# A gated recurrence and a gated convolution on one core: norms kept side by side as word pairs, a written-out order for every engine, and tile-sized loads

## The chip, the cores and the metric

The kernel runs on one NeuronCore of a Trainium2 chip. Its time is the device time of one execution in microseconds (us). A core has five engines that run side by side, each with its own queue of instructions, worked off in order: PE (TensorE, matrix products and transposes), DVE (VectorE), ACT (ScalarE), POOL (GpSimd) and SP (SyncE, which here only issues transfers). Transfers between main memory and the on-chip memory (SBUF) run on 16 DMA engines. PE writes into PSUM[...].

## The reference

There are 4 sequences of 6336 tokens with 256 channels; all inputs and the output are fp32.

```python
a_base = sigmoid(a_param)
a_t    = exp(8 * sigmoid(r_gate) * log(clip(a_base)))
norm   = sqrt(max(1 - a_t * a_t, 1e-6))
h      = a_t[:, t] * h + norm * sigmoid(i_gate) * x     # over t, per sequence
gate   = sigmoid(causal convolution of h, 5 taps per channel)
out    = (gate * (h @ w_val)) @ w_out
```

So each of the 25,344 tokens needs three loads of 256 values, one store of 256 values, a recurrence along the sequence, a convolution and two products with 256x256 matrices.

## The kernel before

**Tiles and chunks.** The tokens of all four sequences stand in one row. A *tile* is 512 tokens (three are 256), a *chunk* is two tiles (some chunks at both ends are one tile). There are 51 tiles and 28 chunks (`CHUNKS`, L17). The 256 channels are two halves of 128, `h` = 0 and 1. Data arrive with tokens on the partitions; the recurrence needs channels on the partitions, so data are transposed on PE.

**One tile's way through the engines.** The names are those of the functions `op_...`:

| step | engine | what it does |
|---|---|---|
| load, loadx | SP | r and i gates, and x, of one chunk |
| tanh | ACT | tanh of half of both gates of a tile, to bf16 `tring` |
| u2 | DVE or POOL | (1 + tanh i) * x to bf16 `uring`; one instruction on DVE (L360), two on POOL (L363, L364); the string `U2` says which |
| srT, exp | PE, ACT | transpose of the r part by half chunk; a = exp(...) to fp32 `aring` |
| e | POOL | a * a to fp32 `ering` (L384) |
| sq | ACT | norm = sqrt(0.25 - 0.25 a * a), bf16, written over `ering` (L388), for one to three chunks at once (`UNITS`) |
| nT, xg | PE, DVE | transpose of the norms back to tokens (L397); `uring` times norm (L404) |
| xT, scan | PE, DVE | transpose of `uring` (L332); the recurrence over a half chunk (L425) |
| conv, tg | PE, ACT | five taps as products with diagonal matrices (L451); tanh (L459) |
| val, gv | PE, DVE | product with w_val (L467); (1 + tanh) * val (L477) |
| out, osb, store | PE, DVE or ACT, SP | product with w_out by 256 tokens (L489); copy from PSUM (L500, L502; the string `OSB` says which); store |

The functions sq and the others on ACT need different tables, so every batch of norms costs a table load before it and one after it (ACT_TABLE_LOAD).

**What sets the order.** The program is made by a planner. `make_jobs` (L110) lists all steps with an engine, a cost (`COST`) and the steps that they wait for. `make_plan` (L160) then goes through time: it takes the step that can start first by these costs, and among equals the one with the lowest `PRIO`. It also hands out the four shared PSUM banks (srT, nT, xT, out). The kernel issues the steps in the order that comes out, so each engine has a fixed queue. SP's queue holds all loads and stores in one order; one that waits for a buffer or for its data holds up all behind it.

**Buffers.** r and i gates: `NIN` = 2 chunks (four tiles); x: `NX` = 3 chunks (six tiles); tanh outputs: `NTR` = 3 and `NTI` = 5 tiles; `ering` 8 tiles, `aring` and `uring` 10, `yring` 6.

**Which tokens lie where.** r is loaded so that a partition holds four neighbouring tokens of a tile, 4 KB in one piece. i and x are loaded with token k * 128 + p on partition p, pieces of 1 KB. The exp turns the order of r into plain token order when it writes `aring`.

Of the kernel before, what the change touches and what calls it, by code (L numbers as in the profile page):

```python
# [9 lines left out]
P = 128  # L10
# [8 lines left out]
UNITS = [1, 2, 2, 3, 3, 3, 3, 3, 2, 2, 1, 3]  # L19
# [4 lines left out]
NIN = 2  # L24
NX = 3
NTR = 3
NTI = 5
# [5 lines left out]
OSB = ("ADDDDDDDDDDDDADDDDDDDDDDDDADDDDDDDDADDDDDDDDDADDDDAADDADDDDDDADDADDDDAADDAAADADADADADADADA"  # L33
       "DAAAAAAAA")

U2 = "PDPDDDDDDPDPDPDPDDPDPPPPPPPPPPPPPPPDPPPPPPPDPPPPPPP"

COST = dict(load=(0.05, 2.8), loadx=(0.02, 1.5), tanh=(0.2, 1.7), u2P=(0.25, 3.15), u2D=(0.2, 1.55), srT=(0.05, 0.45), exp=(0.35, 0.86), e=(0.1, 1.8),
            sq=(0.3, 1.71), nT=(0.05, 0.47), xg=(0.1, 0.58), xT=(0.05, 0.45), scan=(0.21, 2.14), conv=(0.2, 1.1), tg=(0.19, 0.83),
            val=(0.02, 0.93), gv=(0.15, 1.07), out=(0.02, 0.47), osbD=(0.68, 0), osbA=(0.59, 0),  # L40
            store=(0.05, 1.3))
PRIO = dict(load=5.92, loadx=5.97, store=2.53, tanh=6, exp=2.8, sq=0.42, tg=-0.32, srT=-1.6, nT=0.31, xT=3.79,
            conv=5.3, val=4.34, out=2.99, e=5.93, u2=6, xg=4.55, scan=0.36, gv=-0.61, osb=-0.99)
# [66 lines left out]
def make_jobs(sh):  # L110
# [3 lines left out]
    jobs = {op: [] for op in PRIO}  # L114
# [8 lines left out]
    for g, (_, n) in enumerate(sh.tiles):  # L123
        f = n / WIN
        c = sh.chunk_of[g]
        job("tanh", "ACT", f, [("load", c), ("u2", g - NTI)]
            + ([("srT", 2 * sh.chunk_of[g - NTR] + 1)] if g >= NTR else []))
        job("u2", "DVE" if U2[g] == "D" else "POOL", f, [("tanh", g), ("loadx", c)] + ([("xT", 2 * sh.chunk_of[g - NU] + 1)] if g >= NU else []), "u2" + U2[g])
# [7 lines left out]
    for c, (_, n, g0, g1) in enumerate(sh.chunks):  # L136
        f = n / CHUNK
        job("load", "DMA", 2 * f, [("tanh", sh.chunks[c - NIN][3] - 1 if c >= NIN else -1)])
        job("loadx", "DMA", 2 * f, [("u2", sh.chunks[c - NX][3] - 1 if c >= NX else -1)])
# [20 lines left out]
def make_plan(sh):  # L160

    jobs = make_jobs(sh)
    reads = dict(exp="srT", xg="nT", scan="xT", osb="out")
    nxt = dict.fromkeys(jobs, 0)
    done, free, order, mode = {}, dict(DMA=START, ACT=ACT_START), [], "E"
    bank_free, banks = [0.0] * BANKS, {}
    while True:
        best = None  # L170
        for op, todo in jobs.items():
            i = nxt[op]
            if i == len(todo):
                continue
            eng, dur, deps, need = todo[i]
            t = free.get(eng, 0.0)
            if need:
                b = min(bank_free)
                if b == math.inf:
                    continue  # L180
                if b:
                    t = max(t, b + SEM)
            for d in deps:
                e = done.get(d)
                if e is None:
                    break
                if e + SEM > t:
                    t = e + SEM
            else:
                if best is None or (t, PRIO[op]) < best[:2]:  # L190
                    best = (t, PRIO[op], op, i, eng, dur, need)
        if best is None:
            break
        t, _, op, i, eng, dur, need = best
        if eng == "ACT" and op != "osb":
            if (op == "sq") != (mode == "S"):
                dur += TABLE
            mode = "S" if op == "sq" else "E"
        free[eng] = t + dur
        done[op, i] = t + dur + (DMA_LAT if eng == "DMA" else 0.0)  # L200
        if need:
            banks[op, i] = bank_free.index(min(bank_free))
            bank_free[banks[op, i]] = math.inf
        if op in reads:
            bank_free[banks[reads[op], i]] = t + dur
        order.append((t, op, i, eng, dur))
        nxt[op] += 1
    assert all(nxt[op] == len(todo) for op, todo in jobs.items()), nxt
    order.sort(key=lambda o: o[0])
    return order, banks  # L210
# [3 lines left out]
def kernel(  # L214
# [29 lines left out]
    def load(c):  # L244
        t0, nt, g0, g1 = chunks[c]
        nw, nj = g1 - g0, nt // (g1 - g0) // P
        ri = inp.tile([P, 2, 2, SUB, D], FP32, name="ri", tag="ri", bufs=NIN)

        nc.sync.dma_start(ri[:, 0, 0:nw, 0:nj, :], rf[t0:t0 + nt, :].rearrange("(w p j) d -> p w j d", w=nw, j=nj))
        nc.sync.dma_start(ri[:, 1, 0:nw, 0:nj, :].rearrange("p w j d -> p (w j) d"),  # L250
                          if_[t0:t0 + nt, :].rearrange("(k p) d -> p k d", p=P))
        live["ri", c] = ri

    def loadx(c):
        t0, nt, g0, g1 = chunks[c]
        xt = inp.tile([P, 2 * SUB, D], FP32, name="xt", tag="xt", bufs=NX)
        nc.sync.dma_start(xt[:, 0:nt // P, :], xf[t0:t0 + nt, :].rearrange("(k p) d -> p k d", p=P))
        live["xt", c] = xt

    with tc.manual_schedule():  # L260
# [57 lines left out]
        def bank(b, dtype):  # L318
            return psum.tile([P, WIN * 4 // mybir.dt.size(dtype)], dtype, name=f"bank{b}", tag=f"bank{b}", bufs=1)
# [24 lines left out]
        def op_tanh(g, eng):  # L344
# [3 lines left out]
            if g == chunks[c][3] - 1:  # L348
                del live["ri", c]
# [195 lines left out]
```

## Time and profile before

| | |
|---|---|
| median of 13 runs | 319.63 us (317.71 to 324.51) |
| the profiled execution | 317.76 us, span from first to last instruction 316.0 us |
| TensorE clock granted | 0.984 |
| moved | 104.55 MB in 67,327 packets, 54,238 of them between 512 B and 2 KB |
| mean rate of transfers | 331 GB/s; 395 GB/s in the best of 40 slices |
| chain that ended last | ACT 25%, DVE 23%, PE 18%, DMA 17%, issue 12% |
| POOL idle before the square e, waiting for exp | 51.0 us |
| SP waiting for output copies on DVE | 113.2 us |

How to read the lines in the next part. The first lines give, by engine, busy us, share of the span and number of instructions (PEld is the weight loads of PE). A row of 40 digits has the busy share of 40 equal slices of the span in tenths, 9 being 90% or more. A line of the waits reads: engine and line, what it waited for, us in total, number of times, longest. A group of instructions has line, engine, operation, output and inputs, shapes and types, count, then busy us and mean ns of one, then the idle time of the engine just before them and what ended it. A line of the timeline has start, duration, engine, line and operation, and how many instructions were put together. Instructions on one engine overlap a little: the mean of one can be longer than the distance from one start to the next. A busy PE is not a PE at its peak, because the records include the way through the array.

### The profile page before, as it was taken

The page shows a single profiled execution, that of the slowest core. Times are in us where ns is not written, and L with a number is a line of the kernel's source. Part 1 is how long each engine was busy: PE and PEld are TensorE (multiplying, and loading weights), DVE is VectorE, ACT ScalarE, POOL GpSimd, SP SyncE. Part 2 cuts the span into 40 slices and gives each one's busy share as a digit, 9 for nine tenths or more (in the row PEclk, how much of TensorE's full clock was granted, in tenths as well). Part 3 has the DMA queues.
Part 4 walks back from the last instruction along what each step waited for, and adds up shares of the span by engine and source line. Part 5 has one row for each costly group of instructions (what it writes and reads, how often), then busy time and mean ns, then how long its engine had stood idle before and what let it go on. Part 6 is the DMA issues. An engine that isn't in the chain of part 4 may idle for free.

```text
span 316.0 us, 7194 instructions
## 1 busy us (share of the span) xinstructions
PE 243.5 (77%) x2954; PEld 161.5 (51%) x2987; DVE 269.0 (85%) x269; ACT 289.8 (92%) x231; POOL 225.2 (71%) x140
## 2 busy tenths in 40 slices
PE   1273778697578759897989698939977997999994
PEld 1142645454445437554655375617754665655562
DVE  3025598999698989999999999987998999999892
ACT  6689999998979999999999999799989999998963
POOL 6328732879478627999999999999996289868000
PEclk9999998999979999999999999997999999999999
DMA  8999999999999999999999999996999994753334
GB/s 207 345 364 380 367 368 378 378 363 372 389 351 355 375 359 374 350 395 383 375 384 389 391 368 394 392 382 184 394 385 396 383 357 161 247 201 129 136 155 179
DMA packets 67327, 104.55 MB, mean 331 GB/s; under 512 B 3287, under 2 KB 54238, under 8 KB 67294
## 3 DMA queue, kind: packets, MB, share of 16 engines
q1 hardware_dynamic: 65904, 103.82, 92.1%
q0 software_dynamic: 1376, 0.26, 1.0%
q8 instruction: 23, 0.38, 0.5%
q14 instruction: 10, 0.08, 0.1%
q10 hardware_dynamic: 14, 0.01, 0.0%
HBM read 78.39 MB, written 25.95 MB: 330 GB/s over the span
## 4 chain that ended last, share of the span: by engine, by line
ACT 25%; DVE 23%; PE 18%; DMA 17%; issue 12%; SPq 1%; ACTq 0%; DVEq 0%
DVE yring L425 13%; DMA ri<-in_i_gate_dram 12%; ACT tring L351 7%; PE gp L451 6%; DVE gv L477 6%; ACT ering L388 6%; ACT tg L459 5%; PE bank L489 5%; DMA xt<-in_x_dram 3%; ACT aring L376 3%; PE bank L397 3%; PE bank L332 2%; DVE osb L500 2%; ACT L459 2%; ACT L388 2%
## 5 line engine op out<-in xcount | busy, mean ns | idle before, releaser
L384 POOL TENSOR_TENSOR ering<-aring 128x1024 f32<-128x1024 f32 (+2 forms) x56 | 97.7, 1764 | 53.9 <-ACT aring L376 51.0
L425 DVE TENSOR_TENSOR_SCAN yring<-aring,yring,bank 128x1024 bf16<-128x1024 f32 (+5 forms) x54 | 110.0, 2050 | 0.8 <-PE bank L332 0.7
L351 ACT ACTIVATE tring<-ri 128x2048 bf16<-128x2048 f32 (+1 forms) x51 | 93.8, 1869 | 7.5 <-DMA ri<-in_i_gate_dram 6.6
L364 POOL TENSOR_TENSOR uring<-t,xt 128x1024 bf16<-128x1024 f32 (+1 forms) x36 | 83.7, 2324 | 9.4 <-DMA xt<-in_x_dram 5.7
L451 PE MATMUL gp<-yring,diag 64*64 64x512 bf16 (+15 forms) x1196 | 68.4, 350 | 5.8 <-ACT tg L459 3.9
L489 PE MATMUL bank<-wo,gv 128*128 128x256 bf16 x396 | 58.0, 281 | 18.8 <-DVE gv L477 8.5
L477 DVE SCALAR_TENSOR_TENSOR gv<-tg,val 128x1024 bf16<-128x1024 bf16 (+1 forms) x54 | 60.2, 1120 | 7.6 <-ACT tg L459 4.7
L376 ACT ACTIVATE aring<-bank,khf 128x1024 f32<-128x1024 bf16 (+2 forms) x56 | 59.6, 1113 | 2.4 <-PE bank L332 1.7
L459 ACT ACTIVATE tg<-gp 128x1024 bf16<-128x1024 f32 (+1 forms) x51 | 51.2, 1004 | 7.5 <-PE gp L451 7.3
L489 PEld LDWEIGHTS <-gv 128*128 128x128 bf16 x396 | 36.2, 100 | 38.3 <-issue 16.7
L467 PE MATMUL val<-yring,wv 128*128 128x512 bf16 (+1 forms) x171 | 47.1, 379 | 3.1 <-DVE gv L477 1.1
L500 DVE COPY osb<-bank 128x512 f32<-128x512 f32 x69 | 45.4, 677 | 2.7 <-PE bank L489 2.1
L451 PEld LDWEIGHTS <-diag 64*64 64x64 bf16 x1196 | 30.8, 108 | 33.1 <-issue 16.8
L388 ACT ACTIVATE ering<-ering,b 128x2048 bf16<-128x2048 f32 (+4 forms) x15 | 46.7, 3112 | 0.3
L332 PE MATMUL bank<-ident_b,tring 128*128 128x128 bf16 x396 | 30.7, 230 | 18.8 <-ACT tring L351 13.5
L404 DVE TENSOR_TENSOR uring<-bank,uring 128x1024 bf16<-128x1024 bf16 (+1 forms) x51 | 33.3, 667 | 11.4 <-PE bank L397 11.2
L397 PE MATMUL bank<-ident_b,ering 128*128 128x128 bf16 x396 | 31.0, 231 | 15.4 <-ACT ering L388 11.5
L363 POOL TENSOR_SCALAR t<-tring 128x1024 f32<-128x1024 bf16 (+1 forms) x36 | 40.1, 1114 | 2.6 <-ACT tring L351 1.1
L332 PEld LDWEIGHTS <-tring 128*128 128x128 bf16 x396 | 25.5, 103 | 27.9 <-ACT tring L351 15.1
L397 PEld LDWEIGHTS <-ering 128*128 128x128 bf16 x396 | 26.3, 104 | 22.6 <-ACT ering L388 14.2
L332 PE MATMUL bank<-ident_b,uring 128*128 128x128 bf16 x396 | 30.6, 226 | 3.2 <-DVE yring L425 2.0
L332 PEld LDWEIGHTS <-uring 128*128 128x128 bf16 x396 | 25.8, 101 | 9.5 <-issue 6.5
(32 smaller groups left out, 110.0 us busy)
## 6 DMA issues: line engine op xcount, KB each, us to landing
out_dram<-osb SPq DMA_DIRECT2D x48, 512.0 KB, 6.6
ri<-in_r_gate_dram SPq DMA_DIRECT2D x23, 1024.0 KB, 8.0
ri<-in_i_gate_dram SPq DMA_DIRECT2D x23, 1024.0 KB, 10.8
xt<-in_x_dram SPq DMA_DIRECT2D x23, 1024.0 KB, 10.2
ri<-in_r_gate_dram SPq DMA_DIRECT2D x2, 512.0 KB, 7.0
ri<-in_i_gate_dram SPq DMA_DIRECT2D x2, 512.0 KB, 8.3
xt<-in_x_dram SPq DMA_DIRECT2D x2, 512.0 KB, 8.2
ri<-in_r_gate_dram SPq DMA_DIRECT2D x3, 256.0 KB, 3.1
```

Source lines behind the costliest of these rows:

```text
L332: nc.tensor.transpose(out=dst[:, col:col + P], in_=src[:, j, h * P:(h + 1) * P], identity=ident_b[:])
L351: nc.scalar.activation(out=tring[:, r:i + 1:i - r, 0:nj, :], in_=ri[:, :, w, 0:nj, :], func=ACT.Tanh, scale=0.5)
L364: nc.gpsimd.tensor_tensor(out=u, in0=t1, in1=xt, op=ALU.mult)
L376: nc.scalar.activation(out=aring[:, h, a0:a0 + nt].rearrange("c (w p j) -> c w p j", p=P, j=nj), in_=live.pop(("srT", k))[:, 0:nt].rearran ...
L384: nc.gpsimd.tensor_tensor(out=ering[:, h, e0:e0 + nt], in0=a, in1=a, op=ALU.mult)
L388: nc.scalar.activation(out=nring[:, :, 2 * e0:2 * e0 + m], in_=ering[:, :, e0:e0 + m], func=ACT.Sqrt, scale=-0.25, bias=b025[:, 0:1])
L397: nc.tensor.transpose(out=nT[:, j, h * P:(h + 1) * P], in_=nring[:, h, n0 + j * P:n0 + (j + 1) * P], identity=ident_b[:])
L425: nc.vector.tensor_tensor_scan(out=yring[:, h, y0 + c0:y0 + c1], data0=aring[:, h, a0 + c0:a0 + c1], data1=xT[:, c0:c1], initial=0.0 if fr ...
L451: nc.tensor.matmul(out=gp[64 * h:64 * h + 64, m, c0:c1], lhsT=diag[rows, h, kk, rows], rhs=yring[rows, h, src:src + c1 - c0], start=(sh == 0),
L459: nc.scalar.activation(out=tg[:, :, 0:nt], in_=live.pop(("gp", g))[:, :, 0:nt], func=ACT.Tanh, scale=0.5)
L477: nc.vector.scalar_tensor_tensor(out=gv[:, 0:nj, hs, :].rearrange("c j h p -> c j (h p)"), in0=tg[:, hs, 0:nt].rearrange("c h (p j) -> c j ...
L489: nc.tensor.matmul(out=ops[:, e * D:(e + 1) * D], lhsT=gv[:, 2 * i + e, hk, :], rhs=wo[:, hk, :], start=(hk == 0), stop=(hk == H - 1))
```

## The change

The change has four parts.

**Loads by tile, 4 KB in one piece.** load and loadx now take one tile. All three inputs are laid out with four neighbouring tokens on a partition. `NIN` is 3 tiles, `NX` 5 tiles, `NTI` 6. Eight load steps instead of six are issued ahead of everything else.

```diff
-    def load(c):
...
-        nc.sync.dma_start(ri[:, 1, 0:nw, 0:nj, :].rearrange("p w j d -> p (w j) d"),
-                          if_[t0:t0 + nt, :].rearrange("(k p) d -> p k d", p=P))
...
+    def load(g):
+        t0, nt = tiles[g]
+        nj = nt // P
+        ri = inp.tile([P, 2, SUB, D], FP32, name="ri", tag="ri", bufs=NIN)
+        for k, src in enumerate((rf, if_)):
+            nc.sync.dma_start(ri[:, k, 0:nj, :], src[t0:t0 + nt, :].rearrange("(p j) d -> p j d", j=nj))
```

**Pairs of tokens as one fp32 word.** With this layout two neighbouring tokens of a channel can be one 4-byte word. `uring` holds pairs of bf16 values, so u2 writes them interleaved: on DVE as two instructions per tile whose sources alternate between two tokens, on POOL as one instruction whose output steps by two elements. The transposes nT and xT then move fp32 words, four per tile and half instead of eight; nT reads every second word, xT writes every second word. `ering` is one row in which the two halves of a chunk stand one after the other, so that sq works on one contiguous stretch.

```diff
-                nc.vector.scalar_tensor_tensor(out=u, in0=ti, scalar=1.0, in1=xt, op0=ALU.add, op1=ALU.mult)
+                xk = xt.rearrange("p (w e) d -> p w d e", e=2)
+                tk = ti.rearrange("p (w e) d -> p w d e", e=2)
+                for k in range(nj // 2):
+                    nc.vector.scalar_tensor_tensor(out=u[:, k], in0=tk[:, k], scalar=1.0, in1=xk[:, k], op0=ALU.add,
+                                                   op1=ALU.mult)
...
-            nc.gpsimd.tensor_tensor(out=u, in0=t1, in1=xt, op=ALU.mult)
+            nc.gpsimd.tensor_tensor(out=u.rearrange("p w d e -> p w e d"), in0=t1.rearrange("p (w e) d -> p w e d", e=2),
+                                    in1=xt.rearrange("p (w e) d -> p w e d", e=2), op=ALU.mult)
...
-                nc.scalar.activation(out=nring[:, :, 2 * e0:2 * e0 + m], in_=ering[:, :, e0:e0 + m],
+                nc.scalar.activation(out=nring[:, 2 * H * e0:2 * H * e0 + H * m], in_=ering[:, H * e0:H * (e0 + m)],
...
-                for j in range(nt // P):
-                    nc.tensor.transpose(out=nT[:, j, h * P:(h + 1) * P],
-                                        in_=nring[:, h, n0 + j * P:n0 + (j + 1) * P], identity=ident_b[:])
+                for w in range(nw):
+                    nc.tensor.transpose(out=nT[:, w * D + h * P:w * D + (h + 1) * P],
+                                        in_=ering[:, n0 + w:n0 + nw * P:nw], identity=ident_f[:])
...
-            transposes(xT, [(uring[:, g % NU], tiles[g][1] // P) for g in range(*chunks[c][2:])], h)
...
+                for w in range(nw):
+                    nc.tensor.transpose(out=xT[:, at + w:at + nw * P:nw],
+                                        in_=uring_w[:, g % NU, w * D + h * P:w * D + (h + 1) * P], identity=ident_f[:])
```

**The order written out.** `PRIO` and the search in time are gone. Five strings (`ORDER`) give the sequence of steps of each engine, one letter a step, and a sixth (`BANK_ORDER`) the PSUM bank of each step that needs one; `make_plan` only works out start times for them. `UNITS`, `OSB`, `U2` and `COST` have new values.

```diff
-UNITS = [1, 2, 2, 3, 3, 3, 3, 3, 2, 2, 1, 3]
+UNITS = [3, 2, 3, 3, 3, 3, 2, 3, 1, 2, 3]
...
-U2 = "PDPDDDDDDPDPDPDPDDPDPPPPPPPPPPPPPPPDPPPPPPPDPPPPPPP"
+U2 = "DDDPDDPDPPPDPDPDPPPPPPPPPPPPPPPPPPPPPPPPPPPPPPPPPPP"
...
+ORDER = dict(
+    DMA=("lllllxlxlxllxxxlxxlxlxxxlslxllslxxxlxlssxlxlxslsxxssllslxxllxsslsllxsxxxsllslsxlxlsxsllssxxlxlxsxsxl"
...
+    ACT=("tteeetteeettqeetttgeetgeqtegtgteetgeettgqetgetgetteegtetgqgetgetgtegettegetgqgettegetgtegetetgqegett"
```

The counts of instructions that follow from it: table loads on ACT 20 instead of 24 after the setup; square roots 14 instead of 15; output copies 71 on DVE and 28 on ACT instead of 69 and 30; u2 on DVE 17 half-tile instructions (8.5 tiles) instead of 15 tiles; u2 on POOL 42 instead of 36; transposes 396 bf16 and 396 fp32 instead of 1188 bf16; load and store issues 204 instead of 135.

**The factor 0.5 of w_out.** The scaling of `wo` in the setup (L313) is gone; the output copies multiply by 0.5 instead (`tensor_scalar` on DVE, an activation with scale on ACT).

```diff
-        nc.vector.tensor_scalar(out=wo[:], in0=wo[:], scalar1=0.5, scalar2=None, op0=ALU.mult)
...
-                nc.vector.tensor_copy(out=dst, in_=ops[:])
+                nc.vector.tensor_scalar(out=dst, in0=ops[:], scalar1=0.5, scalar2=None, op0=ALU.mult)
             else:
-                nc.scalar.copy(out=dst, in_=ops[:])
+                nc.scalar.activation(out=dst, in_=ops[:], func=ACT.Copy, scale=0.5)
```

## The prediction

> **What bounds the kernel now.** I read the engine shares first, then the slices, then the waits, then single stretches of the timeline.
>
> ```profile
> PE 243.5 (77%) x2954; PEld 161.5 (51%) x2987; DVE 269.0 (85%) x269; ACT 289.8 (92%) x231; POOL 225.2 (71%) x140
> ...
> DVE  3025598999698989999999999987998999999892
> ACT  6689999998979999999999999799989999998963
> ...
> DMA  8999999999999999999999999996999994753334
> ```
>
> Three resources are full at once: ACT from slice 4 to slice 38, the transfers until the last load has landed (about 278 us), DVE from slice 7 to the end. The chain of waits agrees: no engine holds more than a quarter of it (ACT 25%, DVE 23%, PE 18%, DMA 17%). So a saving on one engine counts only as far as the others follow. ACT is the fullest: from its first gate tanh at 5.32 us to the end of its last output copy at 312.60 us are 307.3 us; 289.8 - 2.9 (setup) = 286.9 of them are busy and 20.4 idle. The rest, 3.4 us, is the last store. What ACT waits for:
>
> ```profile
> ACT tg L459 <- PE gp L451: 7.3, 10, 1.8
> ACT tring L351 <- DMA ri<-in_i_gate_dram: 6.6, 4, 3.0
> ```
>
> **What leaves ACT.** The order of the new program has 20 table loads in the main part instead of 24 (11 batches of norms instead of 12, two pairs of them without a switch between; the first batch alone is now three chunks), 28 output copies instead of 30, and 14 square-root instructions instead of 15.
>
> ```profile
> L388 ACT ACT_TABLE_LOAD x12 | 15.4, 1283 | 0.2
> ```
>
> 4 x 1.283 = 5.1; 2 x 0.585 (the mean of ACT's copies) = 1.2; one square-root overhead, about 0.2 (6144 elements take 5.416, 2048 take 2.003, so 0.3 is fixed). ACT sheds 6.5 us. The copy that now also multiplies by 0.5 reads the same 128x512 PSUM tile; I cost it at nothing (the tanh of 1024 elements, 1.030, has a scale too), bounds -0.1 to +0.1 us each, 3 us at most.
>
> **ACT's idle time.** Loads go from a chunk (1 MB each of r and i, two chunks in flight) to a tile (512 KB, three tiles in flight); x from three chunks to five tiles. The largest load wait, 3.0 us before the second tanh, is a wait behind earlier transfers at the start and stays in part. Two more, 1.57 and 1.36 us at 203.8 and 231.5, come out of SP's queue: x loads stand before the gate loads and wait for a buffer.
>
> ```profile
> 204.90 10.61 SPq L257 DMA_DIRECT2D xt<-in_x_dram  x2
> 215.61 2.29 SPq L507 DMA_DIRECT2D out_dram<-osb  x2
> 218.00 0.52 SPq L249 DMA_DIRECT2D ri<-in_r_gate_dram  x1
> ```
>
> With tile-sized buffers a slot is free after one tile instead of two. Against it: 153 load issues instead of 84, at about 0.4 us each 28 us more of SP; SP spent 113 us waiting for output copies alone, so that is hidden. SP is still first in, first out: a store that waits holds the loads behind it. I let 4 us of the 20.4 go, and keep the 7.3 us on the convolution. Bounds: 10 us of idle in all, or 30 if three tiles are too few.
>
> Sum on ACT: 5.3 + (286.9 - 6.5) + 16.4 + 3.4 = **305.5 us of span**.
>
> **What is late next: DVE.** Its first real block starts late, because the first large batch of norms comes late:
>
> ```profile
> 30.46 2.86 ACT L388 ACTIVATE ering<-ering,b 128x3072 bf16<-128x3072 f32 x1
> 36.84 6.92 DVE L425 TENSOR_TENSOR_SCAN yring<-aring,yring,bank 128x512 bf16<-128x512 f32 x4
> ```
>
> In the new order ACT does tanh of tiles 0 to 5 and the exps of chunks 0 to 2 (1.05 + 5 x 1.8 + 1.0 + 1.5 + 2.3 = 14.9 us), then the first batch (1.28 + about 3.2). From 5.3 us, with 3 us of load waits, that is 28 us: xg starts at about 29 instead of 34.4. The early batch of chunk 0 (0.72, with two table loads) is gone, so the few DVE operations before 20 us move to after it; DVE had 10 us idle in 20 to 40. Also gone is the scaling of wo (0.29), before which DVE stood 8.6 us; nothing else was ready then, so I count nothing. 71 output copies instead of 69: +1.4.
>
> u2 on DVE falls from 15 whole tiles to 8.5, but each becomes two instructions whose two sources jump 256 elements at every element:
>
> ```profile
> L360 DVE SCALAR_TENSOR_TENSOR uring<-tring,xt 128x1024 bf16<-128x1024 bf16 x15 | 23.2, 1548 | 7.4 <-DMA xt<-in_x_dram 7.4
> ```
>
> By this row: 8.5 x (1.548 + 0.14 for the second instruction, from xg's 683 and 412 ns) = 14.3, a gain of 8.9. The Trainium skill ("Vector Engine (DVE) Microarchitecture Reference", section 5.2, Measured stream behaviour on trn2) speaks against it: a port keeps its rate only on pairs of adjacent words, and with both sources hopping every element a column takes 1.76 ns instead of 1.05. That is +0.72 us on 1024: 8.5 x 2.41 = 20.5, a gain of 2.7. No row here hops like that on two SBUF sources, so I take 2.7. DVE: 269.0 - 2.7 - 0.3 + 1.4 = 267.4; less about 10 before 29 us, plus 15 idle (18.6 now after 36.8) and 4.6 after its last gv: 29 + 257.4 + 15 + 4.6 = 306. DVE and ACT agree within a microsecond; neither lets the other gain more.
>
> **POOL** takes over 6.5 tiles of u2.
>
> ```profile
> 273.37 3.75 POOL L384 TENSOR_TENSOR ering<-aring 128x1024 f32<-128x1024 f32 x2
> 277.08 1.05 POOL L363 TENSOR_SCALAR t<-tring 128x1024 f32<-128x1024 bf16 x1
> 278.21 2.36 POOL L364 TENSOR_TENSOR uring<-t,xt 128x1024 bf16<-128x1024 f32 x1
> 280.53 1.05 POOL L384 TENSOR_TENSOR ering<-aring 128x512 f32<-128x512 f32 x1
> ```
>
> A tile's u2 takes 280.53 - 277.08 = 3.45, two squares 3.75: +22 us on 225, in gaps (POOL waits 51 us for ACT's exp). From tile 16 on all u2 are POOL's: 2 x 3.45 + 3.75 = 10.65 per chunk, against ACT's 280.4 / 24.75 = 11.3. The cover is thin: 0.34 us per tile. The new write puts bf16 elements 4 bytes apart; reads stay contiguous. No row shows such a write: bounds -0.1 to +1.2 (half of 2.36 more); I take +0.1, since bytes and instruction count stay.
>
> **PE** does 396 transposes of fp32 words in place of 792 of bf16.
>
> ```profile
> 161.95 1.27 PE L451 MATMUL gp<-yring,diag 64*64 64x512 bf16 x20
> 163.16 1.05 PE L489 MATMUL bank<-wo,gv 128*128 128x256 bf16 x8
> 164.04 1.06 PE L332 MATMUL bank<-ident_b,uring 128*128 128x128 bf16 x16
> 164.93 1.06 PE L332 MATMUL bank<-ident_b,tring 128*128 128x128 bf16 x16
> ...
> 3.49 0.28 PEld L305 LDWEIGHTS wc_ps<-ident_f,wrow 5*128 5x128 f32 x2 [1.20 <-DMA wrow<-in_moe_conv_w_dram]
> ```
>
> Start to start, a tile costs 1.21 (conv) + 0.88 (out) + 0.99 (val, from three in 0.74) + 24 x 0.056 = 4.42 us, 219 in all; the 243.5 busy counts latency. The nearest row for fp32 is L305: 0.14 per load of 128 columns. At p = 0.14 a tile is 4.42 - 0.90 + 8 x 0.14 = 4.64, 230 in all, under ACT's 5.66 and hidden. Low end 0.056. High end: the skill ("FP8 and Floating Point Precision", TensorE Precision Notes) has true fp32 as four passes, 4 x 0.056 + 0.14 = 0.36, though "TensorE: Matmul & The Clock Gate" (Terms) calls transpose mode four times faster for fp32. No row streams 128 fp32 columns, so both ends stay; I take 0.14, since L305 is one matmul record per transpose. PE decides from p = 0.27.
>
> **Transfers.** Bytes stay 103.8 MB; i and x packets grow from 1 to 4 KB, r and stores are at 4 KB already. At the best slice rate seen, 395 GB/s, all is moved in 263 us, against 277 at the 375 typical here: enough for ACT's pace (4.19 MB per 11.3 us, 371 GB/s), so I count no gain of its own.
>
> **From span to time.** The profiled execution took 317.76 for a span of 316.0. 305.5 + 1.8 = 307.3, 3.3% less. That execution was the second lowest of the 13; the median, 319.63, scaled alike gives **309.1 us**. Its own range is 302 to 315.
>
> **Rivals.**
> 1. *Nothing gained*: three gate tiles and SP's order make tanh wait for loads where it did not, or the fixed orders wait on each other: idle 26 or more eats the 6.5, giving 315 to 322, say 319. For: SP is blocked for long already. Against: the wait for loads is only 6.6 us now.
> 2. *PE becomes the bound* (the other side): at p = 0.36 a tile costs 6.40, 317 us, plus about 20 of start and drain: 340. It decides from 0.27. For: the pass rule; and the xT transposes write every second word of PSUM, which no matmul of this trace does. Against: L305.
> 3. *POOL becomes the bound*: the 4-byte-step write at +1.2 makes a chunk 13.05; 16 chunks at 1.75 over ACT's pace add 28, less 10 of gain lost anyway: about 333. It decides from +0.34.
>
> **Chances.** Forecast 0.65, first rival 0.15, PE 0.11, POOL 0.09. A measurement here tells about 0.3% from no change, so same is 318.7 to 320.6. Faster: 0.64 + 0.05 = 0.69; same 0.01 + 0.05 = 0.06; slower 0.05 + 0.11 + 0.09 = 0.25. The range 300 to 325 leaves out PE and most of POOL's case.
>
> **What would show it.** Right: ACT about 283 busy with 20 table loads after setup; first scans before 33 us; the fp32 transposes of a tile starting 0.14 apart; the POOL write still near 2.4; u2 halves near 1.2 on DVE. Wrong: PE above 95% with matmul waits in front of xg and scan; POOL without gaps from 100 us on and xg waiting for u2; tanh waiting for loads by more than 10 us in all.

## The result and the profile after

| | before | after |
|---|---|---|
| median | 320.46 us (317.71 to 324.51, 48 runs) | 315.13 us (313.04 to 317.48, 11 runs) |
| after / before | | 0.9855 [0.9823, 0.9886] |
| span of the profiled execution | 316.0 us | 313.7 us |
| span less ACT's busy time | 26.2 us | 30.2 us |

The kernel is 1.45% faster. The forecast was 3.3%, a median of 309.1 us, so the sign is right and less than half of the gain came: 6.0 us are missing. The two profiled executions don't stand alike among their own: the one before, 317.76 us, is the second lowest of 48, the one after, 315.44 us, lies in the middle. So the span after is 8.2 us over the forecast span of 305.5, and some 2 of these 8 are this difference. The busy times first, from the page of the kernel after: the shares of the engines, then the 40 slices of DVE, ACT and the transfers.

```profile
PE 244.2 (78%) x2561; PEld 161.9 (52%) x2591; DVE 267.8 (85%) x272; ACT 283.5 (90%) x224; POOL 240.4 (77%) x152
...
DVE  4014889998989979999799799999898999999983
ACT  5799979799999899999998999999899989977763
...
DMA  7999896999989999999999979999996979433255
```

ACT is 6.3 us less busy than before and the span only 2.3 us shorter: between these two executions 4 us came back as idle time of ACT. By the ratio the time fell by 1.45%, 4.6 us, so over all executions it is about 1.7 us. The rows say where: counted from 0, ACT has 7 in slices 5 and 7 and 8 in slice 13, where it had 9, and 9977763 at the end, where it had 9998963. The same in numbers, from the windows (window, length, then busy us of PE, PEld, DVE, ACT and POOL with the number of instructions, granted clock, share of the DMA engines, GB/s). Before:

```profile
40.00:60.00 20.00, 15.02 (x159) 9.61 (x154) 19.05 (x18) 19.90 (x15) 8.34 (x4) 0.91 1.07 373
...
280.00:300.00 20.00, 19.20 (x220) 12.08 (x224) 18.95 (x19) 18.17 (x23) 8.72 (x11) 1.00 0.33 133
```

After:

```profile
40.00:60.00 20.00, 13.87 (x113) 8.64 (x116) 18.75 (x16) 16.47 (x11) 18.67 (x11) 0.84 0.87 321
...
280.00:300.00 20.00, 19.44 (x189) 11.47 (x191) 18.64 (x18) 14.74 (x19) 5.51 (x7) 1.00 0.35 140
```

Two places: between 40 and 60 us ACT stands for 3.5 us instead of 0.1, and in the tail for 5.3 instead of 1.8. In the tail PE is the fullest engine in both kernels (19.2 and 19.4 of 20 us), so time that ACT saves there need not be time of the kernel. For the first place, the waits of the whole run (what waited for what: us in total, times, longest):

```profile
ACT tring L354 <- DMA ri<-in_i_gate_dram: 8.1, 7, 2.7
...
ACT tg L478 <- PE gp L470: 6.3, 7, 1.9
PE bank L379 <- DVE uring L417: 6.3, 3, 3.3
ACT aring L388 <- PE bank L379: 5.8, 5, 2.4
```

Before, the wait in the fourth line was this:

```profile
ACT aring L376 <- PE bank L332: 1.7, 4, 0.6
```

The waits for gate loads (6.6 us before) did not shrink but grew. And there is a new chain, to be read from the third line to the fourth: the exp (L388) waits for the transpose srT (L379), which waits for xg (L417) on DVE to free the PSUM bank that the written-out bank order gives it. Of its 5.8 us, 4.3 fall between 40 and 60 us; none of the waits for gate loads do. The groups of instructions that the forecast costed:

```profile
L370 POOL TENSOR_TENSOR uring<-t,xt 128x1024 bf16<-128x1024 f32 x40 | 95.3, 2384 | 4.1 <-PE bank L379 0.8
...
L365 DVE SCALAR_TENSOR_TENSOR uring<-tring,xt 128x512 bf16<-128x512 bf16 x17 | 19.8, 1209 | 17.9 <-ACT aring L388 12.6 <-DMA xt<-in_x_dram 5.3
...
L400 ACT ACT_TABLE_LOAD x10 | 12.8, 1283 | 0.2
```

The table loads at L400 and the 10 at three other lines make 20. POOL's write with a step of two costs 2.384 us, as the plain one did (2.420). u2 on DVE costs 1.209 us per half tile in the mean, about what the forecast took.

### The profile page after: what moved, and what is told of

The parts are those of the page before. It is cut to its first block, busy times and chain, and to the rows that moved or that the text cites. A ratio compares the mean times of both kernels' runs of the same rounds, so it can differ in the third digit from the quotient of the medians.

```text
span 313.7 us, 6561 instructions
## 1 busy us (share of the span) xinstructions
PE 244.2 (78%) x2561; PEld 161.9 (52%) x2591; DVE 267.8 (85%) x272; ACT 283.5 (90%) x224; POOL 240.4 (77%) x152
## 4 chain that ended last, share of the span: by engine, by line
PE 15%; DVE 13%; ACT 11%; issue 8%; DMA 5%; SPq 1%; DVEq 0%; ACTq 0%
DMA ri<-in_i_gate_dram 5%; DVE yring L444 5%; PE gp L470 5%; PE bank L508 4%; DVE gv L496 4%; ACT tg L478 3%; ACT ering L400 3%; DVE osb L519 3%; PE val L486 2%; ACT aring L388 1%; PE bank L410 1%; DVE uring L417 1%; PE bank L426 1%; ACT L400 1%; PE bank L379 1%
## 5 line engine op out<-in xcount | busy, mean ns | idle before, releaser
L370 POOL TENSOR_TENSOR uring<-t,xt 128x1024 bf16<-128x1024 f32 (+1 forms) x42 | 97.9, 2331 | 4.2 <-PE bank L379 0.8
L470 PE MATMUL gp<-yring,diag 64*64 64x512 bf16 (+14 forms) x1196 | 67.2, 351 | 4.6 <-ACT tg L478 3.8
L388 ACT ACTIVATE aring<-bank,khf 128x1024 f32<-128x1024 bf16 (+2 forms) x56 | 61.4, 1113 | 5.9 <-PE bank L379 5.8
L379 PE MATMUL bank<-ident_b,tring 128*128 128x128 bf16 x396 | 34.7, 233 | 24.5 <-ACT tring L354 16.7
L519 DVE TENSOR_SCALAR osb<-bank 128x512 f32<-128x512 f32 x71 | 47.5, 678 | 3.3 <-PE bank L508 2.6
L400 ACT ACTIVATE ering<-ering,b 128x4096 bf16<-128x4096 f32 (+3 forms) x14 | 46.0, 3310 | 0.1
L379 PEld LDWEIGHTS <-tring 128*128 128x128 bf16 x396 | 28.2, 104 | 32.3 <-ACT tring L354 18.9
L369 POOL TENSOR_SCALAR t<-tring 128x1024 f32<-128x1024 bf16 (+1 forms) x42 | 43.5, 1036 | 1.7
L410 PE MATMUL bank<-ident_f,ering 128*128 128x128 f32 x198 | 34.2, 304 | 12.2 <-ACT ering L400 10.7
L417 DVE TENSOR_TENSOR uring<-bank,uring 128x1024 bf16<-128x1024 bf16 (+1 forms) x51 | 33.1, 665 | 9.1 <-PE bank L410 7.7
L410 PEld LDWEIGHTS bank<-ident_f,ering 128*128 128x128 f32 x198 | 28.0, 207 | 20.1 <-ACT ering L400 13.2
L426 PE MATMUL bank<-ident_f,uring 128*128 128x128 f32 x198 | 33.9, 295 | 4.3 <-DVE uring L417 1.8
L365 DVE SCALAR_TENSOR_TENSOR uring<-tring,xt 128x512 bf16<-128x512 bf16 x17 | 19.8, 1209 | 17.9 <-ACT aring L388 12.6
```

The source lines that it names most:

```text
L370: nc.gpsimd.tensor_tensor(out=u.rearrange("p w d e -> p w e d"), in0=t1.rearrange("p (w e) d -> p w e d", e=2), in1=xt.rearrange("p (w e) ...
L379: nc.tensor.transpose(out=srT[:, col:col + P], in_=tring[:, g % NTR, j, h * P:(h + 1) * P], identity=ident_b[:])
L388: nc.scalar.activation(out=aring[:, h, a0:a0 + nt].rearrange("c (w p j) -> c w p j", p=P, j=nj), in_=live.pop(("srT", k))[:, 0:nt].rearran ...
L400: nc.scalar.activation(out=nring[:, 2 * H * e0:2 * H * e0 + H * m], in_=ering[:, H * e0:H * (e0 + m)], func=ACT.Sqrt, scale=-0.25, bias=b0 ...
L410: nc.tensor.transpose(out=nT[:, w * D + h * P:w * D + (h + 1) * P], in_=ering[:, n0 + w:n0 + nw * P:nw], identity=ident_f[:])
L470: nc.tensor.matmul(out=gp[64 * h:64 * h + 64, m, c0:c1], lhsT=diag[rows, h, kk, rows], rhs=yring[rows, h, src:src + c1 - c0], start=(sh == 0),
```

## The experiments

After the result there were three theories of what is missing: **(a)** ACT does not set the pace alone, so its 6.5 us are worth less than 6.5; **(b)** three gate tiles in flight are too few, and the loads keep ACT waiting; **(c)** the pairs cost more than they bring, through u2 on DVE and what waits behind it.

### What a microsecond of ACT or of DVE is worth

Thirteen small instructions were added to one engine, evenly over the run, each on a tile of its own that nobody else uses.

```diff
+            if g % 4 == 2:
+                nc.scalar.activation(out=apad[:], in_=apad[:], func=ACT.Copy, scale=0.5)
```
```diff
+            if g % 4 == 2:
+                nc.vector.scalar_tensor_tensor(out=dpad[:], in0=dpad[:], scalar=1.0, in1=dpad[:], op0=ALU.add, op1=ALU.mult)
```

> The changed kernel with 13 more activations of 128x512 on ACT (about 0.55 us each, 7 us in all, one behind the tanh of every fourth tile), which gives back what ACT shed. Theory (DVE sets the pace from 29 us on, ACT only follows): 0 to 2 us slower than the changed kernel, so 315 to 317. Rival (ACT still sets the pace): 5 to 7 us slower, 320 to 322.

> The changed kernel with 13 more operations of 128x512 on DVE (about 0.65 us each, 8 us in all, one behind every fourth gv). Theory (DVE sets the pace): 6 to 9 us slower, 321 to 324. Rival (ACT sets the pace): 0 to 2 us slower.

> The changed kernel beside the three others on one chip: 315 us, ratio to the kernel before 0.985.

| kernel | busy of the engine | time / before |
|---|---|---|
| after, run again beside them | ACT 283.6, DVE 267.5 us | 0.9851 [0.9792, 0.9911] |
| 13 operations more on ACT | ACT 290.3 us (+6.7) | 0.9941 [0.9905, 0.9977] |
| 13 operations more on DVE | DVE 282.9 us (+15.4) | 1.0152 [1.0091, 1.0213] |

ACT: 0.0090 of 320.26 us (before, in these runs) is 2.9 us for 6.7 us of work, 0.43 per us. The expectation had 0 to 2 us if DVE sets the pace and 5 to 7 if ACT does; 2.9 is neither. DVE: 0.0301 is 9.6 us for 15.4 us, 0.63 per us. The two intervals of each difference, put together, leave ACT between 0.1 and 0.8 and DVE between 0.45 and 0.8: both are under one, and which is dearer stays open. The operations on DVE took 1.197 us in the mean, twice ACT's, and POOL's busy time rose with them from 240.7 to 244.5 us, so their price holds some of POOL's; the last section tells why. Counted by the 8.9 us that the 13 operations take undisturbed, a microsecond put on DVE costs 1.08 us. The groups of the two kernels:

```profile
L483 ACT ACTIVATE apad<-apad 128x512 bf16<-128x512 bf16 x13 | 8.2, 632 | 0.0
```
```profile
L504 DVE SCALAR_TENSOR_TENSOR dpad<-dpad 128x512 bf16<-128x512 bf16 x13 | 15.6, 1197 | 0.0
```

So (a) holds for time that is added. If time taken away counts alike, which no run tried, what the forecast took for 6.5 us is some 2.8 us by the middle value.

### The order, the fourth tile, the piece size and the pairs, one by one

The change was taken apart into four switches. *No pairs* puts the bf16 transposes and the contiguous u2 of before into the kernel after:

```diff
-            u = uring[:, g % NU, 0:nj * D].rearrange("p (w d e) -> p w d e", d=D, e=2)
+            u = uring[:, g % NU, 0:nj * D].rearrange("p (j d) -> p j d", d=D)
...
-                for w in range(nw):
-                    nc.tensor.transpose(out=xT[:, at + w:at + nw * P:nw],
-                                        in_=uring_w[:, g % NU, w * D + h * P:w * D + (h + 1) * P], identity=ident_f[:])
-                at += nw * P
+                for j in range(tiles[g][1] // P):
+                    nc.tensor.transpose(out=xT[:, at:at + P], in_=uring[:, g % NU, j * D + h * P:j * D + (h + 1) * P],
+                                        identity=ident_b[:])
+                    at += P
```

*1 KB* loads i and x as before, a token at a time (`"(j p) d -> p j d"` in place of `"(p j) d -> p j d"`). *Four tiles* is `NIN = 4` instead of 3. What is left with no pairs, 1 KB and three tiles is the written-out order with tile-sized loads, the other buffers and the moved factor, called the order in what follows. And the reverse of one switch: 4 KB pieces in the kernel before.

> The kernel before with i and x loaded in 4 KB pieces as r is, all else as it was. Tokens of i and x then lie in another order than the transposes assume: that part of the computation is changed. Theory (ACT and DVE in turn set the pace, transfers only where a load is waited for; 6.6 us of load waits in all): 0 to 3 us faster, 317 to 320. Rival (the transfers set the pace, and packet size is what the change brought): 4 to 6 us faster, like the whole change.

> The changed kernel with i and x loaded in 1 KB pieces, all else the same (tokens of i and x lie in another order than the pairs assume: that part of the computation is changed). Theory: 0 to 3 us slower than the changed kernel, 315 to 318. Rival (packet size brought the gain): 4 to 6 us slower, back at 320.

> The changed kernel, order and 4 KB loads kept, with bf16 transposes (eight per tile and half) and contiguous u2 (one instruction per tile on DVE); i and x stay in neighbour order while the norms are in block order, so that part of the computation is changed. Theory (a u2 on DVE waits for POOL's two-input instruction once per instruction, so 8 fewer instructions save up to 8 stalls of about 1 us; PE costs the same, 8 x 0.056 against 4 x 0.11): 1 to 4 us faster than the changed kernel, 311 to 314. Rival (the fp32 transposes are what the change gained from): 2 us or more slower.

> The changed kernel with four gate tiles in flight instead of three. Theory (the wait of tanh for loads, 8 us, is mostly the start and the order in SP's queue): under 2 us faster. Rival (three tiles are too few): tanh's load wait falls below 4 us and the time by 3 to 5 us, to 310 to 312.

> The changed kernel's order, tile-sized loads and buffers alone: i and x in 1 KB pieces, bf16 transposes, contiguous u2; tokens as in the kernel before. From the runs so far: 1 KB loads cost 2.6% and pairs 0.6% in this order. Theory (the gain came from the 4 KB loads, the order with three gate tiles loses by itself): 0.5% slower than the kernel before, 0 to 1.2%, 320 to 324. Rival (the order is the gain, the 1 KB run was slow for another reason): 1% or more faster than before.

> The same with four gate tiles in flight. Theory (with 1 KB pieces the transfers are near their limit and three tiles leave them idle too often): 1 to 2% faster than the order alone, so 0.985 to 0.997 of the kernel before. Rival (depth is not what the order suffers from): under 0.5% from the order alone.

> The changed kernel with bf16 transposes, contiguous u2, 4 KB pieces and four gate tiles in flight: both suspected losses taken out (i and x stay in neighbour order while the norms are in block order, so that part of the computation is changed). Theory (the parts add: -0.45 - 1.6 - 1.0): 0.966 to 0.972 of the kernel before, 309 to 311. Rival (4 KB pieces and depth cure the same waits and do not add): 0.977 to 0.981, no faster than either alone.

| pairs | pieces | gate tiles | time / before | span less ACT busy | ACT's wait for gate loads |
|---|---|---|---|---|---|
| before | 1 KB | 2 chunks | 1 | 26.2 us | 6.6 us |
| before | 4 KB | 2 chunks | 0.9936 [0.9891, 0.9981] | 27.8 us | 2.4 us |
| no | 1 KB | 3 | 0.9955 [0.9921, 0.9989] | 32.0 us | 14.3 us |
| no | 1 KB | 4 | 0.9821 [0.9768, 0.9874] | 29.2 us | 9.9 us |
| no | 4 KB | 3 | 0.9792 [0.9734, 0.9849] | 28.0 us | 10.6 us |
| no | 4 KB | 4 | 0.9610 [0.9565, 0.9654] | 22.3 us | 3.8 us |
| yes | 1 KB | 3 | 1.0111 [1.0064, 1.0158] | 36.7 us | 13.7 us |
| yes | 4 KB | 3 (the change) | 0.9855 [0.9823, 0.9886] | 30.2 us | 8.1 us |
| yes | 4 KB | 4 | 0.9784 [0.9732, 0.9836] | 28.5 us | 4.5 us |

ACT's busy time is 282.7 to 284.1 us in the seven rows of the new order: they differ in how long ACT stands. The last two columns are from one execution each: a second profile of the kernel after has 32.1 us and 9.6 us, so differences of 2 us there say little. A path from before to after, in points of the time before: the order with three tiles -0.5%, the pairs +1.6%, the 4 KB pieces -2.6%. Each switch, at each setting of the others:

- **4 KB pieces**: -1.6%, -2.1% (no pairs, three and four tiles), -2.6% (pairs), and only -0.6% in the kernel before. They are the largest gain of the change.
- **A fourth gate tile**: -1.3%, -1.8%, and -0.7% with the pairs (that one alone is at the edge of its interval). Three tiles cost, so (b) holds.
- **The pairs**: +1.6%, +0.6%, +1.7%. The second (4 KB and three tiles, as in the change) is inside its interval, the others are not: (c) holds, in the change itself by the middle value only.

Four of these expectations missed. The 1 KB pieces cost 8.2 us, more than even their rival had. The order alone is 0.5% faster, where theory had it slower and the rival 1% faster. The fourth tile's 2.3 us and 4.5 us of waits lie between theory and rival. And the kernel with both losses taken away gained more (0.961) than the sum of the parts (0.966 to 0.972).

SyncE's queue shows (b) directly. Its waits in the kernel after, then with `NIN = 4` (L262 issues the gate loads; it waits for the tanh that frees the tile):

```profile
SPq L262 <- ACT tring L354: 73.3, 30, 7.5
```
```profile
SPq L262 <- ACT tring L354: 25.3, 14, 4.2
```

In the kernel before this wait was 32.5 us. Everything behind it in the queue, x loads and stores, stands too. Not all that the fourth tile takes away is gone: SyncE's wait for output copies on DVE rises from 72.6 to 87.2 us. The kernel with both losses taken away (no pairs, four tiles) on its page:

```profile
PE 241.9 (79%) x2950; PEld 162.0 (53%) x2987; DVE 262.7 (86%) x264; ACT 282.7 (93%) x224; POOL 243.5 (80%) x152
```

and in its waits:

```profile
ACT tring L354 <- DMA ri<-in_i_gate_dram: 3.8, 4, 2.6
...
ACT aring L383 <- PE bank L374: 2.3, 3, 1.2
```

The wait of exp for its transpose fell from 5.8 to 2.3 us, and it is the pairs that it follows: 1.7 to 2.4 us in the four kernels of the table that have none, 5.8 to 6.7 us in the three that have them. The median of this kernel, 308.45 us, is near the forecast of 309.1: the order and the large pieces give as much as was predicted of the change, and the three tiles and the pairs took half of it away. There is luck in that agreement, because 2.1% come from the pieces, for which the forecast counted nothing. With the tokens in the order that its expectation tells, this kernel measures a cost and is no version to use.

How the pairs cost time is seen at one place. The timeline of the kernel after (start, duration, engine, line, operation, in brackets the idle time before it and what ended it):

```profile
35.97 3.01 DVE L365 SCALAR_TENSOR_TENSOR uring<-tring,xt 128x512 bf16<-128x512 bf16 x2
36.04 2.38 POOL L396 TENSOR_TENSOR ering<-aring 128x1024 f32<-128x1024 f32 x1
...
38.90 1.27 DVE L417 TENSOR_TENSOR uring<-bank,uring 128x1024 bf16<-128x1024 bf16 x2
...
39.63 1.01 PE L379 MATMUL bank<-ident_b,tring 128*128 128x128 bf16 x8 [2.08 <-DVE uring L417]
...
40.68 1.20 ACT L388 ACTIVATE aring<-bank,khf 128x1024 f32<-128x1024 bf16 x1 [1.51 <-PE bank L379]
```

And with no pairs and four tiles:

```profile
35.46 1.56 DVE L362 SCALAR_TENSOR_TENSOR uring<-tring,xt 128x1024 bf16<-128x1024 bf16 x1
...
35.90 2.88 POOL L391 TENSOR_TENSOR ering<-aring 128x1024 f32<-128x1024 f32 x1
...
36.95 1.28 DVE L412 TENSOR_TENSOR uring<-bank,uring 128x1024 bf16<-128x1024 bf16 x2
...
37.66 2.30 ACT L383 ACTIVATE aring<-bank,khf 128x1024 f32<-128x1024 bf16 x2
37.68 0.61 PE L374 MATMUL bank<-ident_b,tring 128*128 128x128 bf16 x8 [0.33 <-DVE uring L412]
```

The u2 of one tile takes 3.01 us in two halves and 1.56 in one. In the first view POOL's square (36.04 to 38.42 us) gets in between the two halves, and the second ends 0.56 us after it; in the second view the square has to wait for the one instruction, and takes 2.88 us. xg is behind u2, the bank comes free later, srT stands 2.08 us instead of 0.33, and ACT stands 1.51 us. Over the whole run DVE is busier with the pairs by 3.4 us (267.8 against 264.4, three tiles) and by 6.0 us (268.7 against 262.7, four); at 0.63 per us that is an estimate of 2.1 and 3.8 us, against 2.0 and 5.6 us measured (0.6% and 1.7%). By the middle values DVE's own time explains most of it, at four tiles not all.

### Does ACT's time count more once the waits are gone?

The thirteen operations of ACT went into the kernel without pairs and with four tiles (the same part of the computation is changed).

> The same with the 13 extra activations on ACT, 6.7 us. Theory (ACT shares the pace with DVE and PE whatever the loads do): 2 to 4 us slower than without, as in the changed kernel. Rival (in the changed kernel the load waits hid part of it, and without them ACT counts in full): 5.5 to 7 us slower.

Measured: 0.9678 [0.9636, 0.9720] against 0.9610 [0.9565, 0.9654], with ACT busy 288.8 us instead of 282.7. 0.0068 of 321.11 us is 2.2 us for 6.1, 0.36 per us, between 0.05 and 0.7 by the intervals, not told apart from the 0.43 above. So the full price of the rival is ruled out: even where ACT is busy 93% of the span, a good part of what is added to it disappears.

### Three attempts to save what was lost

*Reads in order.* On DVE the source is read token by token and the write steps by two, as on POOL.

```diff
-                    nc.vector.scalar_tensor_tensor(out=u[:, k], in0=tk[:, k], scalar=1.0, in1=xk[:, k], op0=ALU.add,
+                    nc.vector.scalar_tensor_tensor(out=uk[:, k], in0=tk[:, k], scalar=1.0, in1=xk[:, k], op0=ALU.add,
```

> The changed kernel with u2 on DVE reading in order and writing with a step of two bf16 elements, instead of sources that jump at every element. Theory (DVE sets the pace, and a half tile of u2 costs 1.2 us because of the jumps): a half tile falls to 0.7 to 0.9 us, DVE sheds 5 to 8 us, the time falls by 3 to 6 us to 309 to 312. Rival (ACT or the loads set the pace): under 1 us.

Measured: 0.9829 [0.9773, 0.9885] against 0.9851 of the kernel after in the same runs, no difference. The shortest instruction takes 710 ns where the alternating reads take 684, so the alternating reads weren't what u2 paid for.

*One instruction per tile.* Four tokens side by side instead of two, `NIN = 4`: u2 on DVE is one instruction, and the transposes pick every second word.

```diff
-            u = uring[:, g % NU, 0:nj * D].rearrange("p (w d e) -> p w d e", d=D, e=2)
+            u = uring[:, g % NU, 0:nj * D].rearrange("p (d j) -> p d j", j=nj)
...
-                                        in_=uring_w[:, g % NU, w * D + h * P:w * D + (h + 1) * P], identity=ident_f[:])
+                                        in_=uring_w[:, g % NU, h * P * nw + w:(h + 1) * P * nw:nw], identity=ident_f[:])
```

> The changed kernel with four gate tiles in flight and u2 on DVE as one instruction per tile: the four tokens of a channel lie side by side, so that the words for the transposes stand two apart in SBUF, and nT writes every second word as xT does. Theory (each u2 instruction on DVE can wait once for a two-input instruction of POOL; 8 fewer instructions save 4 to 8 us on DVE, at the 0.6 us per us that the DVE run showed): 1 to 4 us faster than four tiles alone, 309 to 312. Rival (the step of 8 bytes in POOL's write costs more than 2.5 us per tile and POOL becomes the bound): slower, 320 or more; POOL's second instruction then shows 3 us or more.

Measured: 0.9734 [0.9684, 0.9783], the fastest kernel here that computes the reference. It isn't told apart from four tiles with pairs (0.9784), whose interval overlaps. It did not work in the way it was meant to: u2 on DVE takes 21.4 us in all, and 21.1 us there, and POOL's write with a step of four costs 2.62 us instead of 2.38 (the rival needed 3). The waits did shrink: exp waits 3.2 us for its transpose instead of 6.7. Both versions beat the kernel before and the kernel after in their middle values, and four tiles are a change of one digit.

*Copies in the tail.* Four late output copies moved from DVE to ACT, which stands in the tail, with `NIN = 4`: four letters of `OSB` and of the two strings of `ORDER`.

> The changed kernel with four gate tiles in flight and four of the last output copies moved from DVE to ACT, which waits 13 us after 280. Theory (DVE and PE set the pace of the tail, ACT has room): 1 to 2.5 us faster than four tiles alone, 310 to 312. Rival (PE alone sets the tail): within 0.5 us of it.

Measured: 0.9794 [0.9744, 0.9844] against 0.9784: nothing gained. That fits PE, the fullest engine of the tail in the windows above, as what sets the pace there. This idea fell.

## Why the prediction was right in sign and too large

**Right.**
- *ACT's work.* 283.5 us busy, about 283 forecast, with 20 table loads after the setup; the copies with the factor cost 597 ns on ACT (585 before) and 678 on DVE (677 before).
- *The start.* The first scan is at 29.92 us (asked for: before 33), xg at 28.92 (about 29).
- *PE.* The timeline of the kernel after has transposes in rows of eight: norms (L410) and x (L426) as fp32 words, and, for comparison, r (L379) as bf16.

```profile
82.38 1.23 PE L410 MATMUL bank<-ident_f,ering 128*128 128x128 f32 x8 [2.50 <-ACT ering L400]
...
85.49 1.04 PE L426 MATMUL bank<-ident_f,uring 128*128 128x128 f32 x8
```
```profile
109.47 0.61 PE L379 MATMUL bank<-ident_b,tring 128*128 128x128 bf16 x8
```

One record alone takes 0.28, 0.27 and 0.22 us (the medians of these lines), so in these rows seven starts take the rest: 0.135, 0.11 and 0.056 us apart. The forecast took 0.14 for fp32, and PE would have decided from 0.27. The estimate by four passes ("FP8 and Floating Point Precision", TensorE Precision Notes), 0.36 us, isn't seen here, and writing every second word of PSUM (L426) takes no longer than L410's write of words side by side. PE's busy time is 244.2 us, before 243.5.
- *POOL.* The write with a step costs 2.384 us, and the bound where POOL decides was 0.34 above 2.36.

**Wrong: the idle time.** This is the step that failed. The sum on ACT was 5.3 + 280.4 busy + 16.4 idle + 3.4. With the measured 280.6 busy in the main part (283.5 less 2.9) and 3.1 us after ACT's last copy, the span of 313.7 leaves 313.7 - 5.3 - 280.6 - 3.1 = 24.7 us idle. The forecast said: *"I let 4 us of the 20.4 go"*. It rose by 4 instead. By what ACT waited for:

| ACT's wait for | before | forecast | after |
|---|---|---|---|
| gate loads | 6.6 us | 2.6 | 8.1 |
| the transpose in front of exp | 1.7 | no term | 5.8 |
| the convolution | 7.3 | 7.3 | 6.3 |

The first row misses by 5.5 us, the second by 4.1, the third by -1.0: 8.6 in all, against 24.7 - 16.4 = 8.3 (some 2 of them lie in the low execution before). Two causes are behind the rows:

1. *Three tiles.* The step argued from "With tile-sized buffers a slot is free after one tile instead of two", and it put the case that three tiles are too few at 30 us of idle. Runs: the waits for gate loads rose, SyncE stood 73.3 us for a free gate tile, and a fourth tile brought the waits to 4.5 us and was worth 0.7 to 1.8%. Finer tiles free earlier, but three tiles in flight hold less than the four that two chunks held. The forecast named both sizes and didn't compare them. Its own sign for this case, over 10 us of waits for loads, was not reached and would have missed the loss.
2. *The pairs.* The forecast costed u2 as DVE time only (a gain of 2.7 us) and no wait behind it. Runs: +0.6 to +1.7% of time, by a busier DVE and the chain u2, xg, srT, exp; without the pairs the wait in the second row is 1.7 us at the same three tiles.

**Wrong: the worth of ACT's time.** The forecast took 6.5 us of ACT as 6.5 us of time, although it had said that "a saving on one engine counts only as far as the others follow". The added operations price it at 0.43 per us in the middle, 2.8 us. "DVE and ACT agree within a microsecond" should have been a warning that neither counts in full. This is the same missing time seen from another side, not more to add to it.

**Wrong: DVE.** The sum was 29 + 257.4 + 15 + 4.6 = 306, with "less about 10 before 29 us". DVE was busy 6.9 us before 29, not 10, so 260.9 remain after it; and 23.8 us of idle and tail follow instead of 19.6 (the 18.6 us of idle that the forecast read before are 17.6 by the windows). That is 3.5 + 4.2 us more, 313.7. The u2 part of it was near: 19.8 us measured, 20.5 taken. That was luck; the last section shows why.

**Wrong: the pieces.** *"I count no gain of its own"* for the 4 KB pieces. They gave 1.6 to 2.6% in the new order. In the kernel before they give only 0.6%. So the term that the forecast left out is the largest of the change. It argued from the best rate seen before, 395 GB/s; no slice with 1 KB pieces is over 400, and with 4 KB pieces the best is 419, in the kernel before as in the change. Each tile also lands sooner. From issue to landing (the last number, a median in us), in the kernel after and then with 1 KB pieces, where r still has 4 KB:

```profile
ri<-in_r_gate_dram SPq DMA_DIRECT2D x48, 512.0 KB, 6.4
ri<-in_i_gate_dram SPq DMA_DIRECT2D x48, 512.0 KB, 7.7
```
```profile
ri<-in_r_gate_dram SPq DMA_DIRECT2D x48, 512.0 KB, 7.4
ri<-in_i_gate_dram SPq DMA_DIRECT2D x48, 512.0 KB, 8.4
```

ACT waits less for its loads (10.6 us against 14.3 without pairs, 8.1 against 13.7 with them). Why the pieces are worth three times as much in the new order stays open. In the kernel before, too, the large pieces bring the wait for gate loads down, from 6.6 to 2.4 us, but the wait for the convolution rises from 7.3 to 11.7; that is one execution each and no cause.

The first rival, idle that eats the gain (315 to 322 us, "say 319"), was half true at the same time: the result, 315.1, lies at its lower end and at the upper end of the forecast's own range, and the order with three tiles and 1 KB pieces gives 0.5% alone.

## What to carry to other kernels

Count what is in flight in bytes when tiles get finer: three tiles of a half chunk are less cover than two chunks, and the queue of loads shows it as a wait for the buffer. Where two engines are near full together, price a microsecond of each by adding some operations to it before crediting a saving; here it was about 0.4 for the fuller and 0.6 for the other, whose added operations were themselves held up. A layout that saves instructions on an engine with room can be a loss when it splits an instruction on the engine that others wait for.

## What the runs showed of the hardware

**DVE and POOL take turns.** In these runs a DVE operation with two inputs in SBUF that starts while POOL runs a TENSOR_TENSOR doesn't run beside it. Timeline of the kernel with added operations on DVE:

```profile
60.22 2.38 POOL L372 TENSOR_TENSOR uring<-t,xt 128x1024 bf16<-128x1024 f32 x1
...
61.43 1.71 DVE L504 SCALAR_TENSOR_TENSOR dpad<-dpad 128x512 bf16<-128x512 bf16 x1
...
62.54 2.35 POOL L398 TENSOR_TENSOR ering<-aring 128x1024 f32<-128x1024 f32 x1
```

POOL ends at 62.60 and DVE at 63.14, 0.54 us later. The same gap is at 97.84 and 98.38, and at 296.04 and 296.59. Undisturbed the operation takes 683 ns; here 1.71, 2.14 and 1.78 us. POOL waits in turn: its next square (L398) ends 1.75 us after DVE's operation and takes 2.35 us instead of 1.89. The Trainium skill ("GPSIMD Engine Reference", specs) names the shared SBUF interfaces and the contention with DVE instructions with two SBUF inputs; in these runs it is the whole rest of the other's operation. An operation of DVE with one input in PSUM isn't held: gv beginning at 60.23 beside the same POOL instruction took 1.29 us, and 1.21 at 95.11 (1.21 is its mean in the kernel after). This is why 13 operations cost 15.6 us instead of 8.9 (13 x 683 ns), and why u2 has a mean of 1.209 us: the median is 702 ns, the longest 2.854. The trace before has it already:

```profile
24.53 4.72 POOL L384 TENSOR_TENSOR ering<-aring 128x1024 f32<-128x1024 f32 x2 [5.44 <-ACT aring L376]
...
28.27 2.06 DVE L360 SCALAR_TENSOR_TENSOR uring<-tring,xt 128x1024 bf16<-128x1024 bf16 x1 [0.77 <-DMA xt<-in_x_dram]
```

Two squares alone take 3.75 us and a u2 that meets none takes 1.20 to 1.21 in this trace, so the mean of 1.548 us that the forecast took as the price of u2 holds waits for POOL.

**Which hops cost.** Three forms of u2 on one tile, at a time when POOL stands: with pairs (two instructions, sources alternating between two tokens), with four tokens side by side (one instruction, sources going through four), and contiguous (one instruction).

```profile
26.59 1.31 DVE L365 SCALAR_TENSOR_TENSOR uring<-tring,xt 128x512 bf16<-128x512 bf16 x2 [2.19 <-DMA xt<-in_x_dram]
```
```profile
26.75 1.97 DVE L362 SCALAR_TENSOR_TENSOR uring<-tring,xt 128x1024 bf16<-128x1024 bf16 x1 [1.90 <-DMA xt<-in_x_dram]
```
```profile
26.60 1.23 DVE L362 SCALAR_TENSOR_TENSOR uring<-tring,xt 128x1024 bf16<-128x1024 bf16 x1 [2.61 <-DMA xt<-in_x_dram]
```

Alternating between two runs shows no cost beyond that of a second instruction (1.31 against 1.23 us), and going through four costs 0.74 us. The rule that the forecast took ("Vector Engine (DVE) Microarchitecture Reference", section 5.2, 1.76 ns a column where both sources hop) gives an estimate of 1.80 us for 1024 columns: that is near the four-token form, and it isn't seen with two. So the forecast charged nearly the right total, 20.5 us, to the wrong cause: the hop between two shows no cost, and the waiting for POOL makes up for it. The four-token form has one instruction less to hold up, and gives back in hops what it gains.
